# Tokens of a block in another order: turned query tiles loaded in runs of 512 bytes

## The chip, the core and the metric

The kernel runs on one core of a Trainium2 chip. The metric is the time of one execution on the device in microseconds (us); several runs of the same program are taken, and their median stands for the kernel. A difference of 0.2% (some 3.2 us here) is about the least that such a measurement can tell from none.

## What is computed

Linear attention on 8 batches x 8 heads x 576 tokens x 64 channels, then two MLPs on the 4608 x 512 tokens, all in float32:

```python
q_s = exp(q - max(q, -1)); q_s = q_s / (sum(q_s, -1) + 1e-9)
k_s = exp(k - max(k, 2));  k_s = k_s / (sum(k_s, 2) + 1e-9)
kv  = einsum('bhsd,bhse->bhde', k_s, v)
x   = einsum('bhsd,bhde->bhse', q_s, kv)     # then (token, head*64+channel), 4608 x 512
h = x @ w_in;   g = h * clip(h + 3, 0, 6) / 6;  x = g @ w_out      # first MLP, 512 -> 2048 -> 512
h = x @ w2_in;  g = h * sigmoid(h);             out = g @ w2_out   # second MLP
```

## The kernel before

The 4608 tokens are 9 blocks of 512 (`BLK`). A unit u is one block and one pair of heads, so 36 units, four per block. A block's tokens lie on the 128 partitions with four tokens each: partition p holds tokens 4p to 4p+3 (`i` in the code, `NCH` = 4). A block does not end where a batch ends (576 tokens), so `parts(j)` gives block j as one or two ranges of partitions, p0 to p0+n, each with its own batch; n is a multiple of 16.

For each unit the queries go through a softmax over the channels (`q_max`, `q_sub`, `q_exp`, `q_sum`, `q_norm`), are turned so that channels lie on partitions, and are multiplied with the batch's 128 x 128 matrix `kv` (`x_mm`, L495). The result `px` has channels on partitions and the block's 512 tokens as columns; it is the MLP's input. Up to here a token's column number is 128 i + p. Each matmul of `x_mm` reads and writes the columns of one range of partitions for all four i, as a pattern of 4 x n columns. As weights and columns are full float32, one such instruction of the program stands in the trace as two MATMUL records, each with its weight load.

The queries are turned in two ways. Units 0 to 8 use four transposes on TensorE and a copy on ACT (`q_turn`, `q_copy` L486). Units 9 to 35 use `q_blocks` (L469), a transpose on DVE that turns each 32 x 32 square in place, then `q_store` (L473), which writes the tile to DRAM (`zd`), and `q_load` (L479): four loads of 32 partitions each bring the squares to their places. In each load, one of 32 partitions takes 16 runs of 32 floats (128 bytes).

The MLPs are matmuls in which tokens stay columns: `mm1` (L541, first product), a gate on ACT and DVE (`Gate`), `mm2` (L613, L615). The first MLP of most blocks and all the attention run up to 720 us. From 720 to 1485 us five pairs of blocks go through a seven-product scheme (`inner` L1340, `outer` L1499), whose results leave over `turn_blocks` and, for the last pair, `turn_last`: DVE transposes of 32 x 32 squares and four stores each (L1547 to L1552, L1567 to L1572). The last block's second MLP is written plainly, and in its end `tail` (L637 to L652) the roles are changed: the gate's output is the weight, so a result tile has 128 tokens on partitions. `tail` makes four such tiles c, copies each in two halves (DVE and ACT, L651) and stores each half, 128 rows of 1 KB, from the queue of SP or of ACT (L652). Nothing comes after these eight stores.

The order of the work is made when the program is built: jobs with engine, guessed time and key go to the planner (`Plan`) in `middle`, events by time in `second_mlp`. Each engine then runs its list in order, and SP issues nearly all DMAs from one list; a wait there holds up what is queued behind it.

Quoted here is the one line that says how the rows of `out` belong to the columns of a tile in `tail`:

```python
rows = out[j * BLK : (j + 1) * BLK, :].rearrange("(p i) d -> i p d", i=NCH)
```

Of the kernel before, what the change touches and what calls it, by code (L numbers as in the profile page):

```python
# [18 lines left out]
P = 128  # L19
BLK = 512  # L20
# [3 lines left out]
def f32(ap):  # L24
    return ap.bitcast(F32)
# [3 lines left out]
def efficient_attention_then_two_mlps(  # L29
# [11 lines left out]
    nc = tc.nc  # L41
# [7 lines left out]
    NCH = BLK // P  # L49
# [32 lines left out]
    zd = dram.tile([NB * NP, P, NCH * P], F32, name="zd")  # L82
# [90 lines left out]
    def slot(o, i, part):  # L173
        if part == "A21":
            return 7 * NPR + i
        if o:
            return OUTER.index(part) * NPR + i
        if part == "A22":
            return 6 + 7 * i + 2 if i < NPR - 1 else 7 * NPR - 1
        return (0 if i == 0 else 6 + 7 * (i - 1)) + INNER.index(part) + (  # L180
            1 if i and part not in INNER[:2] else 0
        )
# [105 lines left out]
    qt, kv = {}, {}  # L288
    xt = {}
    live = {}  # L290
# [39 lines left out]
    def parts(j):  # L330
        p = 0
        while p < P:
            b, s = divmod(j * BLK + NCH * p, S)
            n = min(P - p, (S - s) // NCH)
            yield p, n, b, s
            p += n

    def a_psum(shape, small=False):
        t = ps_a.tile([P, 512], F32, tag="a", name="pa")
        return t  # L340
# [116 lines left out]
    def q_turn(u):  # L457
        t = live.pop(("qe", u)).rearrange("p i h d -> p i (h d)")
        pq = a_psum(None)
        for i in range(NCH):  # L460
            nc.tensor.transpose(pq[:, i * P : (i + 1) * P], t[:, i, :], ident)
        live["pq", u] = pq
# [3 lines left out]
    def q_blocks(u):  # L466
        e = live.pop(("qe", u)).rearrange("p i h d -> p (i h d)")
        z = tmp.tile([P, NCH * P], F32, tag="t2k", name="qz")
        nc.vector.transpose(z, e)  # L469
        live["z", u] = z  # L470

    def q_store(u):
# [1 line left out]

    def q_load(u):
        t = att.tile([P, NCH * P], F32, tag="qT", bufs=1, name="qt")
        zb = zd[u].rearrange("(a i) (c b k) -> b i c a k", a=4, b=4, c=NCH)
        for b in range(4):
            nc.sync.dma_start(  # L479
                t[b * 32 : b * 32 + 32].rearrange("i (c a k) -> i c a k", c=NCH, a=4), zb[b]  # L480
            )
        live["pq", u] = t

    def q_copy(u):
        t = att.tile([P, NCH * P], F32, tag="qT", bufs=1, name="qt")
        nc.scalar.copy(t, live["pq", u])  # L486
        live["pq", u] = t

    def x_mm(u):
        j, pr = divmod(u, NP)  # L490
        qt = live.pop(("pq", u)).rearrange("p (i n) -> p i n", i=NCH)
        px = a_psum(None)
        pv = px.rearrange("p (i n) -> p i n", i=NCH)
        for p0, n, b, _ in parts(j):
            nc.tensor.matmul(  # L495
                pv[:, :, p0 : p0 + n], kv[b, pr], qt[:, :, p0 : p0 + n],
                start=p0 == 0, stop=True, skip_group_check=True,
            )
        live["px", u] = px

    def x_upper(u):
# [135 lines left out]
    def tail(s):  # L637

        ph, j, f = s
        g, w = gt.pop(s), wo[ph, f]  # L640
        rows = out[j * BLK : (j + 1) * BLK, :].rearrange("(p i) d -> i p d", i=NCH)
        for c, y in enumerate(acc.pop((ph, j))):
            cs = slice(c * P, (c + 1) * P)
            for n, (a, e) in enumerate(((0, 0), (1, 0), (0, 1))):
                nc.tensor.matmul(y, g[:, e, cs], w[:, a, :], start=False, stop=n == 2)
            o = tmp.tile([P, 512], F32, tag="t2k", name="o")
            for h, (copy, eng) in enumerate(
                ((nc.vector.tensor_copy, nc.sync), (nc.scalar.copy, nc.scalar))
            ):
                half = slice(h * 256, (h + 1) * 256)  # L650
                copy(o[:, half], y[:, half])  # L651
                eng.dma_start(rows[c][:, half], o[:, half])  # L652

    def x_store(u):
        j, pr = divmod(u, NP)
# [37 lines left out]
    for i, u in enumerate(range(2, NP)):  # L693
        o = i * (KB + VB + QB)
# [15 lines left out]
    def a_pool():  # L710
        return a_psum(None)
# [109 lines left out]
    for j in range(1, NB):  # L821
        for pr in range(NP):
            n = (j - 2) * NP + pr
            begin[j * NP + pr] = 3 * pr if j == 1 else NF - 3 + int(3.3 * n) + LATE[n]

    def first_block():
# [30 lines left out]
        def unit(u, key, until=7):  # L857
# [25 lines left out]
            kx = add("ACT", 0.75, key(3), lambda: k_exp(u), [kb])  # L883
            qt_ = add("PE", 0.65, key(3), turning("q_turn", u, lambda: q_turn(u)), [qn], ["a"], [qe])
            ql = add("ACT", 0.6, key(3), lambda: q_copy(u), [qt_], ["qT"], ["a"])
            pkb = f"y{u}" if small else "a"
            mm = add(
# [4 lines left out]
            va = add("DVE", 0.35, key(4), lambda: kv_sum(u), [mm])  # L892
            vl = add("ACT", 0.65, key(4), lambda: kv_scale(u), [va], [], [pkb])
            xm = add("PE", 1.0, key(5), turning("x", u, lambda: x_mm(u)), [ql, vl], ["a"], ["qT"])
            xu = add("ACT", 0.6, key(5), lambda: x_upper(u), [xm])
            if u in DIRECT_X:
# [94 lines left out]
    def middle():  # L991
# [12 lines left out]
        def unit(u):  # L1004
# [28 lines left out]
            if u < DIRECT:  # L1033
                qt_ = add("PE", 0.65, key(3), lambda: q_turn(u), [qn], ["a"], ["qe"])
                ql = add("ACT", 0.62, key(3), lambda: q_copy(u), [qt_], ["qT"], ["a"])
            else:
                qb = add("DVE", 0.72, key(3), lambda: q_blocks(u), [qn], ["t2k"], ["qe"])
                z0 = dma(0.35, key(3), lambda: q_store(u), 256, [qb], [], ["t2k"])
                ql = dma(1.4, key(4), lambda: q_load(u), 256, [z0], ["qT", "z"])
# [269 lines left out]
    def second_mlp(last):  # L1309
# [4 lines left out]
        for _ in range(2):  # L1314
            t = raw.tile([P, 2, BLK], F32, tag="raw", name="fin")
            fixed += [t[:, 0], t[:, 1]]
        whole = xs.tile([P, 4, 2, DM], F32R, tag="x", name="ring")
# [5 lines left out]
        def small(name, tag="t2k"):  # L1323
            return tmp.tile([P, BLK], F32, tag=tag, bufs=1 if tag == "r" else 5, name=name)
# [4 lines left out]
        d = {}  # L1329
# [96 lines left out]
        def split_tile(x=False):  # L1426
            n = 2 + turns[0] % 3 if x else turns[0] % 5
            turns[0] += 1
            if n == 4:
                return [  # L1430
                    att.tile([P, BLK], F32R, tag=tag, bufs=1, name="gsp") for tag in ("ke", "qe")
                ]
            if n == 2:
                return [
                    att.tile([P, BLK], F32R, tag="sp", bufs=3, name="gsp") for _ in range(2)
                ]
            if n < 2:
                t = gs.tile([P, 2, BLK], F32R, tag="g", name="gsp")
            else:
                t = att.tile([P, 2, BLK], F32R, tag="qT", bufs=1, name="gsp")  # L1440
            return [t[:, 0], t[:, 1]]
# [94 lines left out]
        turned = []  # L1536

        def turn_blocks(j, k, part):


            h, n = (1, k) if k < NC else (0, k - NC)
            a, m = divmod(n, 2)
            x = fixed[4 * m + ((3, 1), (0, 2))[a][h]]
            if part == 0:
                if not turned:
                    turned.extend(split_tile())
                nc.vector.transpose(f32(turned[0]), x)  # L1547
            o = f32(turned[0])
            rows = out[(j + h) * BLK : (j + h + 1) * BLK, n * P : (n + 1) * P]
            e = slice(part * 32, part * 32 + 32)  # L1550
            nc.sync.dma_start(
                rows[:, e].rearrange("(b r i) c -> r i b c", b=4, i=NCH),  # L1552
                o[e].rearrange("r (i b c) -> r i b c", i=NCH, b=4),
            )
            if part == 3:
                turned.pop(0)
# [3 lines left out]
        def turn_last(j, k):  # L1560

            h, n = (1, k) if k < NC else (0, k - NC)
            a, m = divmod(n, 2)
            x = fixed[4 * m + ((3, 1), (0, 2))[a][h]]
            o = gone.pop() if k else small("o2")
            gone.append(x)
            nc.vector.transpose(o, x)  # L1567
            rows = out[(j + h) * BLK : (j + h + 1) * BLK, n * P : (n + 1) * P]
            for i in range(4):
                e = slice(i * 32, i * 32 + 32)  # L1570
                nc.sync.dma_start(
                    rows[:, e].rearrange("(b r i) c -> r i b c", b=4, i=NCH),  # L1572
                    o[e].rearrange("r (i b c) -> r i b c", i=NCH, b=4),
                )
# [4 lines left out]
        for b, (ph, j) in enumerate(PASSES):  # L1579
            t0 = T  # L1580
            place = {}
            for n in range(NPR):
                at = place[n] = {}
# [7 lines left out]
            start = {}  # L1591
# [4 lines left out]
            for n in range(NPR):  # L1596
                pair_events(b, n, place[n])
                for p, t in place[n].items():
                    k = 7 * NPR * b + slot(0, n, PAIR[p][0]) // 2
                    uses[k] = max(uses.get(k, 0.0), t)  # L1600
            for u in range(7 * NPR):
                p, i = KEYS[u // NPR], u % NPR
                t = start[u]
# [7 lines left out]
                k = 7 * NPR * b + 7 * NPR // 2 + u // 2  # L1611
# [49 lines left out]
    with tc.manual_schedule(engines=None):  # L1661
        nc.gpsimd.memset(ident, 1.0)
        nc.gpsimd.affine_select(
            out=ident, in_=ident, compare_op=ALU.is_equal, fill=0.0, base=0,
# [50 lines left out]
```

## Time and profile before

| what | value |
|---|---|
| median of 3 runs | 1578.06 us (1576.75 to 1578.68) |
| profiled execution, its own time | 1579.01 us |
| its span, first to last instruction | 1577.0 us |
| TensorE busy | 1558.9 us, 99% of the span |
| VectorE, ScalarE, GpSimd busy | 70%, 48%, 31% |
| granted clock of TensorE, mean | 1.000 |
| DMA queue of SP and ACT: packets, data, share of 16 engines | 389,040, 340.32 MB, 70.3% |

A profile shows one execution. PE is TensorE's matmuls, PEld its weight loads, DVE VectorE, ACT ScalarE, POOL GpSimd, SP the engine that issues DMAs. Busy time of an engine that is not the bottleneck costs nothing by itself; what counts is what the work that ends last waits for.

### The profile page before, as it was taken

What the parts mean: (1) busy time and instruction counts of PE and PEld (TensorE: products, weight loads), DVE (VectorE), ACT (ScalarE), POOL (GpSimd) and SP (SyncE); (2) the same over time, 40 slices, a digit from 0 to 9 for tenths busy, and PEclk for the clock granted to TensorE, in tenths of its full rate; (3) what the DMA queues carried; (4) which work ended last, traced back from release to release, by engine and by line L of the source; (5) the groups of instructions that cost most, each with busy time, mean ns of one, the idle gap of its engine ahead of it and who ended that gap; (6) DMA issues with size and microseconds to landing.
All of it is one profiled execution on the core that took longest, in us unless ns stands there. A gap on an engine that the chain in (4) does not pass through costs nothing.

```text
span 1577.0 us, 22414 instructions
## 1 busy us (share of the span) xinstructions
PE 1558.9 (99%) x7352; PEld 1268.4 (80%) x7352; DVE 1111.1 (70%) x1792; ACT 761.6 (48%) x1360; POOL 487.8 (31%) x442
## 2 busy tenths in 40 slices
PE   7999999999999999999999999999999999999998
PEld 4777878887878888888888888888888888888887
DVE  7988577776767776554689569846986697677632
ACT  6886245454555554443365236533643464345322
POOL 4334224433424335321232243323223422440000
PEclk9999999999999999999999999999999999999999
DMA  9915977777778875755666786766668875879850
GB/s 267 345 44 185 313 216 227 238 215 215 223 215 246 235 227 166 238 174 193 192 222 218 214 226 224 249 217 192 237 203 218 220 252 192 227 226 370 260 127 27
DMA packets 391203, 342.82 MB, mean 217 GB/s; under 512 B 184880, under 2 KB 297520, under 8 KB 391088
## 3 DMA queue, kind: packets, MB, share of 16 engines
q1 hardware_dynamic: 389040, 340.32, 70.3%
q8 instruction: 58, 0.95, 0.2%
q10 hardware_dynamic: 2048, 1.08, 0.2%
q14 instruction: 57, 0.47, 0.1%
HBM read 247.20 MB, written 94.11 MB: 216 GB/s over the span
## 4 chain that ended last, share of the span: by engine, by line
PE 92%; DMA 2%; issue 1%; DVE 1%; POOL 1%; ACT 1%; SPq 1%; ACTq 0%; POOLq 0%; DVEq 0%
PE pb L1340 24%; PE pb L1499 24%; PE h L541 20%; PE y L613 17%; PE y L615 3%; PE pa L495 2%; PE pa L397 2%; DMA qraw<-in_q_dram 1%; DMA xr<-xq 0%; DMA xq<-xq 0%; POOL wi L164 0%; SPq L232 0%; PE pa L368 0%; PE pa L356 0%; ACT r L554 0%
## 5 line engine op out<-in xcount | busy, mean ns | idle before, releaser
L541 PE MATMUL h<-x,wi 128*128 128x512 f32 x1536 | 382.5, 396 | 1.6 <-POOL wi L164 0.9
L1340 PE MATMUL pb<-xo,ring 128*128 128x512 f32 x1680 | 383.0, 389 | 0.0
L1499 PE MATMUL pb<-gsp,ring 128*128 128x512 f32 x1680 | 382.4, 389 | 0.0
L1340 PEld LDWEIGHTS pb<-xo,ring 128*128 128x128 f32 x1680 | 315.4, 188 | 65.8 <-issue 0.5
L1499 PEld LDWEIGHTS pb<-gsp,ring 128*128 128x128 f32 x1680 | 315.4, 188 | 65.4
L541 PEld LDWEIGHTS h<-x,wi 128*128 128x128 f32 x1536 | 283.5, 188 | 65.9 <-POOL wi L164 2.0
L613 PE MATMUL y<-g,wo 128*128 128x512 f32 x1344 | 323.9, 390 | 0.6 <-ACT g L569 0.6
L613 PEld LDWEIGHTS y<-g,wo 128*128 128x128 f32 x1344 | 251.4, 188 | 53.6 <-ACT g L569 1.1
L1327 DVE TENSOR_TENSOR gsp<-g,gsp 128x512 fp32r<-128x512 f32 x240 | 183.0, 782 | 26.0 <-ACT gsp L1445 25.2
L1445 ACT CAST gsp<-g 128x512 fp32r<-128x512 f32 x240 | 143.6, 621 | 106.2 <-PE pb L1499 88.3
L578 DVE SCALAR_TENSOR_TENSOR h<-r,h 128x512 f32<-128x512 f32 x112 | 77.4, 691 | 80.3 <-ACT r L554 80.1
L554 ACT ACTIVATE r<-h 128x512 f32<-128x512 f32 x112 | 67.0, 598 | 133.4 <-PE h L541 131.7
L1327 POOL TENSOR_TENSOR xst<-xst 128x512 f32<-128x512 f32 x32 | 72.1, 2254 | 167.4 <-DVE xo L1327 85.3
L1327 DVE TENSOR_TENSOR g<-r,pb 128x512 f32<-128x512 f32 x96 | 65.7, 684 | 54.6 <-ACT r L1354 54.1
L1354 ACT ACTIVATE r<-pb 128x512 f32<-128x512 f32 x96 | 57.1, 595 | 97.0 <-DVE pb L1327 72.8
L1327 POOL TENSOR_TENSOR g<-g 128x512 f32<-128x512 f32 x40 | 53.6, 1340 | 148.6 <-DVE g L1327 123.4
L1327 POOL TENSOR_TENSOR s<-U,s 128x512 f32<-128x512 f32 x32 | 42.6, 1331 | 173.1 <-DVE U L1327 173.1
L569 ACT CAST g<-h 128x512 fp32r<-128x512 f32 x112 | 65.6, 586 | 59.8 <-DVE h L578 51.5
L572 DVE TENSOR_TENSOR g<-h,g 128x512 fp32r<-128x512 f32 x97 | 66.7, 688 | 28.8 <-ACT g L569 27.3
L1327 DVE TENSOR_TENSOR U<-pb,s 128x512 f32<-128x512 f32 x80 | 55.0, 688 | 17.0 <-PE pb L1340 14.9
L194 POOL TENSOR_TENSOR fa<-fa 128x256 f32<-128x256 f32 x64 | 49.9, 780 | 43.7 <-DVE sp L226 28.5
L427 POOL TENSOR_TENSOR qe<-qraw,qm 128x512 f32<-128x512 f32 x34 | 37.9, 1114 | 79.4 <-DVE qz L469 46.0
(158 smaller groups left out, 1721.2 us busy)
## 6 DMA issues: line engine op xcount, KB each, us to landing
ring<-ws SPq DMA_DIRECT2D x280, 512.0 KB, 3.9
ws<-sp SPq DMA_DIRECT2D x256, 128.0 KB, 2.6
wi_early<-in_moe_w_in_dram SPq DMA_DIRECT2D x16, 512.0 KB, 8.6
wo_early<-in_moe_w_out_dram SPq DMA_DIRECT2D x16, 512.0 KB, 9.6
wi_raw<-in_moe_w_in_dram SPq DMA_DIRECT2D x16, 512.0 KB, 5.0
ws<-w_sum SPq DMA_DIRECT2D x64, 128.0 KB, 2.2
ws<-fa SPq DMA_DIRECT2D x64, 128.0 KB, 2.3
wo_raw<-in_moe_w_out_dram SPq DMA_DIRECT2D x16, 512.0 KB, 4.4
```

Of the source, the lines that this page charges most:

```text
L194: lambda to=to, x=x, y=y, op=op: nc.gpsimd.tensor_tensor(out=at[to], in0=at[x], in1=at[y], op=op)
L541: nc.tensor.matmul(h, w[:, a, c, :], x[:, e, c, :], start=(c == 0 and n == 0), stop=(c == NC - 1 and n == 2),)
L554: nc.scalar.activation(self.r, self.h, AF.Relu, bias=3.0)
L569: nc.scalar.copy(self.g[:, 0], self.r)
L572: nc.vector.tensor_tensor(out=self.g[:, 1], in0=self.r, in1=f32(self.g[:, 0]), op=ALU.subtract)
L578: nc.vector.scalar_tensor_tensor(out=self.h, in0=self.r, scalar=6.0, in1=self.h, op0=ALU.min, op1=ALU.mult)
L613: nc.tensor.matmul(y[c], w[:, a, cs], g[:, e, :], start=st, stop=sp)
L1327: (eng or nc.vector).tensor_tensor(out=out, in0=a, in1=b, op=how)
L1340: nc.tensor.matmul(to, ws_[:, a], e[:, c], start=p in ("P1", "P6", "P5") and c == 0 and m == 0, stop=c == 1 and m == 2, skip_group_check=True,
L1354: nc.scalar.activation(r, d[b, n, key], AF.Sigmoid)
L1445: nc.scalar.copy(t[0], source(p, i))
L1499: nc.tensor.matmul(d[b, p][m], w[:, a, m * P : (m + 1) * P], t[e], start=new and i == 0 and k == 0, stop=i == NPR - 1 and k == 2, skip_gro ...
```

## The change

A token's column is no longer 128 i + p. With p = 32 a + n, it is 128 a + 32 i + n: the four groups of 32 partitions come one after the other, and the four tokens of a partition stand 32 columns apart.

- `q_blocks` writes its 32 x 32 squares in the new order (pattern 4 x 4 x 32 in place of 512 elements in a row), and each load of `q_load` has 4 runs of 128 floats (512 bytes) for a partition in place of 16 runs of 32. `q_copy` gets the same reordering for units 0 to 8.
- A range of partitions p0 to p0+n is now a stretch of columns in a row as far as it takes whole groups of 32, and a pattern of 4 x 16 columns where it begins or ends in the middle of a group. `columns` gives these pieces, and `x_mm` issues one matmul for each.
- The transposes in `turn_blocks` and `turn_last` undo the order (input and output patterns 4 x 4 x 32); their stores are as before.
- `tail`: a tile c now holds group a = c, with 32 i + y on its partitions, so a store goes to rows 128 c + 4 y + i: a pattern of 4 x 32 rows in place of 128 rows with one step.

```diff
@@ -335,6 +335,19 @@
             yield p, n, b, s
             p += n
 
+    def columns(p0, p1):
+        whole = -(-p0 // 32), p1 // 32
+        out = []
+        if whole[0] < whole[1]:
+            out.append(lambda t: t[:, whole[0] * P : whole[1] * P])
+        if p0 % 32:
+            a, y = divmod(p0, 32)
+            out.append(lambda t: t[:, a * P : (a + 1) * P].rearrange("p (i y) -> p i y", i=NCH)[:, :, y:32])
+        if p1 % 32:
+            b, z = divmod(p1, 32)
+            out.append(lambda t: t[:, b * P : (b + 1) * P].rearrange("p (i y) -> p i y", i=NCH)[:, :, 0:z])
+        return out
+
     def a_psum(shape, small=False):
         t = ps_a.tile([P, 512], F32, tag="a", name="pa")
         return t
@@ -466,7 +479,9 @@
     def q_blocks(u):
         e = live.pop(("qe", u)).rearrange("p i h d -> p (i h d)")
         z = tmp.tile([P, NCH * P], F32, tag="t2k", name="qz")
-        nc.vector.transpose(z, e)
+        nc.vector.transpose(
+            z.rearrange("p (b i c) -> p i b c", b=4, i=NCH), e.rearrange("p (i b c) -> p i b c", b=4, i=NCH)
+        )
         live["z", u] = z
 
     def q_store(u):
@@ -474,28 +489,29 @@
 
     def q_load(u):
         t = att.tile([P, NCH * P], F32, tag="qT", bufs=1, name="qt")
-        zb = zd[u].rearrange("(a i) (c b k) -> b i c a k", a=4, b=4, c=NCH)
+        zb = zd[u].rearrange("(a x) (b n) -> b x a n", a=4, b=4)
         for b in range(4):
-            nc.sync.dma_start(
-                t[b * 32 : b * 32 + 32].rearrange("i (c a k) -> i c a k", c=NCH, a=4), zb[b]
-            )
+            nc.sync.dma_start(t[b * 32 : b * 32 + 32].rearrange("x (a n) -> x a n", a=4), zb[b])
         live["pq", u] = t
 
     def q_copy(u):
         t = att.tile([P, NCH * P], F32, tag="qT", bufs=1, name="qt")
-        nc.scalar.copy(t, live["pq", u])
+        nc.scalar.copy(
+            t.rearrange("p (a i n) -> p i a n", a=4, i=NCH),
+            live["pq", u].rearrange("p (i a n) -> p i a n", a=4, i=NCH),
+        )
         live["pq", u] = t
 
     def x_mm(u):
         j, pr = divmod(u, NP)
-        qt = live.pop(("pq", u)).rearrange("p (i n) -> p i n", i=NCH)
+        qt = live.pop(("pq", u))
         px = a_psum(None)
-        pv = px.rearrange("p (i n) -> p i n", i=NCH)
         for p0, n, b, _ in parts(j):
-            nc.tensor.matmul(
-                pv[:, :, p0 : p0 + n], kv[b, pr], qt[:, :, p0 : p0 + n],
-                start=p0 == 0, stop=True, skip_group_check=True,
-            )
+            for at in columns(p0, p0 + n):
+                nc.tensor.matmul(
+                    at(px), kv[b, pr], at(qt),
+                    start=p0 == 0, stop=True, skip_group_check=True,
+                )
         live["px", u] = px
 
     def x_upper(u):
@@ -638,7 +654,7 @@
 
         ph, j, f = s
         g, w = gt.pop(s), wo[ph, f]
-        rows = out[j * BLK : (j + 1) * BLK, :].rearrange("(p i) d -> i p d", i=NCH)
+        rows = out[j * BLK : (j + 1) * BLK, :].rearrange("(a y i) d -> a i y d", a=4, i=NCH)
         for c, y in enumerate(acc.pop((ph, j))):
             cs = slice(c * P, (c + 1) * P)
             for n, (a, e) in enumerate(((0, 0), (1, 0), (0, 1))):
@@ -649,7 +665,7 @@
             ):
                 half = slice(h * 256, (h + 1) * 256)
                 copy(o[:, half], y[:, half])
-                eng.dma_start(rows[c][:, half], o[:, half])
+                eng.dma_start(rows[c][:, :, half], o[:, half])
 
     def x_store(u):
         j, pr = divmod(u, NP)
@@ -1544,7 +1560,10 @@
             if part == 0:
                 if not turned:
                     turned.extend(split_tile())
-                nc.vector.transpose(f32(turned[0]), x)
+                nc.vector.transpose(
+                    f32(turned[0]).rearrange("p (i b c) -> p b i c", i=NCH, b=4),
+                    x.rearrange("p (b i c) -> p b i c", i=NCH, b=4),
+                )
             o = f32(turned[0])
             rows = out[(j + h) * BLK : (j + h + 1) * BLK, n * P : (n + 1) * P]
             e = slice(part * 32, part * 32 + 32)
@@ -1564,7 +1583,10 @@
             x = fixed[4 * m + ((3, 1), (0, 2))[a][h]]
             o = gone.pop() if k else small("o2")
             gone.append(x)
-            nc.vector.transpose(o, x)
+            nc.vector.transpose(
+                o.rearrange("p (i b c) -> p b i c", i=NCH, b=4),
+                x.rearrange("p (b i c) -> p b i c", i=NCH, b=4),
+            )
             rows = out[(j + h) * BLK : (j + h + 1) * BLK, n * P : (n + 1) * P]
             for i in range(4):
                 e = slice(i * 32, i * 32 + 32)
```

No instruction changes places with another on any engine; pieces are added and patterns changed. On PE, a unit of block 3 (ranges of 48 and 80 partitions), before, with `kv` of the two batches (pa is `px`, pa<-vbuf,ke the next unit's product of keys and values, h<-x,wi the first MLP):

```order
L541 MATMUL h<-x,wi 128x512 x12
L495 MATMUL pa<-qt,kv_96 128x4x48
L495 MATMUL pa<-qt,kv_95 128x4x80
L397 MATMUL pa<-vbuf,ke 64x65 x10
L541 MATMUL h<-x,wi 128x512 x9
```

And in the changed kernel:

```order
L557 MATMUL h<-x,wi 128x512 x12
L511 MATMUL pa<-qt,kv_96 128x128
L511 MATMUL pa<-qt,kv_96 128x4x16
L511 MATMUL pa<-qt,kv_95 128x256
L511 MATMUL pa<-qt,kv_95 128x4x16
L410 MATMUL pa<-vbuf,ke 64x65 x10
L557 MATMUL h<-x,wi 128x512 x9
```

Two matmuls have become four, with as many columns in all. Over the program there are 24 more: one more for each of the four units of blocks 1 and 7, two more for each of blocks 3 and 5, none elsewhere.

On SP, the loads of one unit, before and then in the changed kernel, with the store of the next unit's tile ahead:

```order
L473 DMA zd<-qz 128x512
L635 DMA yd<-o 128x512
L479 DMA qt<-zd 32x16x32 x4
L635 DMA yd<-o 128x512
```

```order
L488 DMA zd<-qz 128x512
L651 DMA yd<-o 128x512
L494 DMA qt<-zd 32x4x128 x4
L651 DMA yd<-o 128x512
```

The queue is the same; the four loads move the same bytes in a quarter of the runs.

On ACT, the end of the program (half of the last stores; the other four are on SP), before and then in the changed kernel:

```order
L651 COPY o<-y_13836 128x256
L652 DMA out_dram<-o 128x256
L651 COPY o<-y_13837 128x256
L652 DMA out_dram<-o 128x256
```

```order
L667 COPY o<-y_13860 128x256
L668 DMA out_dram<-o 4x32x256
L667 COPY o<-y_13861 128x256
L668 DMA out_dram<-o 4x32x256
```

The place is the same; the outermost step of the store's target has 4 entries where it had 128.

## Rows read from the trace of the kernel before

**Rows 1.** Chain of work that ended last, whole program, shares of the span.

```profile
PE 92%; DMA 2%; issue 1%; DVE 1%; POOL 1%; ACT 1%; SPq 1%; ACTq 0%; POOLq 0%; DVEq 0%
```

**Rows 2.** Windows: us, busy time of each engine (instructions), granted clock, DMA share, GB/s.

```profile
148.00:350.00 202.00, 201.56 (x1051) 162.67 (x1050) 143.37 (x261) 95.46 (x176) 74.53 (x89) 1.00 0.81 243
350.00:370.00 20.00, 19.37 (x101) 15.44 (x101) 10.29 (x20) 9.06 (x18) 10.73 (x12) 1.00 0.75 223
...
420.00:470.00 50.00, 47.40 (x241) 37.91 (x240) 35.19 (x64) 25.15 (x47) 21.91 (x25) 1.00 0.70 212
470.00:600.00 130.00, 130.00 (x672) 105.20 (x672) 95.63 (x172) 67.57 (x122) 51.14 (x58) 1.00 0.77 227
...
720.00:1485.00 765.00, 765.00 (x3375) 633.29 (x3374) 564.19 (x825) 349.43 (x614) 221.65 (x144) 1.00 0.74 231
```

**Rows 3.** Chain of work around three units' `x_mm`: start us, us, what.

```profile
652.29 0.86 PE pa L495 x2
653.15 2.75 PE h L541 x12
...
303.32 0.86 PE pa L495 x4
304.18 2.73 PE h L541 x12
...
562.75 0.92 PE pa L495 x4
563.68 2.79 PE h L541 x12
```

**Rows 4.** The same, where ten matmuls of L397 follow `x_mm`.

```profile
338.45 0.86 PE pa L495 x4
339.31 0.88 PE pa L397 x20
...
603.52 0.92 PE pa L495 x4
604.44 0.88 PE pa L397 x20
```

**Rows 5.** Lines of SP's queue, DMA issues: duration ns min/median/max, first and last start us.

```profile
L479 SPq DMA_DIRECT2D qt<-zd x108: 557/634/1432, 188.4 to 700.7; - x108
L473 SPq DMA_DIRECT2D zd<-qz x27: 319/407/589, 163.6 to 632.4; - x27
L206 SPq DMA_DIRECT2D ws<-wi x24: 576/614/1170, 137.7 to 162.3; - x24
```

**Rows 6.** Chain of work before PE's longest wait, and that wait (timeline).

```profile
451.25 0.64 SPq L479
...
452.65 2.79 DMA yd<-o
...
464.19 0.30 PE L356 MATMUL pa<-ident,peaks 128*128 128x128 f32 x1 [2.07 <-DVE peaks L351]
```

**Rows 7.** Lines of the transposes and of a DVE operation with exchanged axes: ns min/median/max.

```profile
L469 DVE STREAM_TRANSPOSE qz<-qe x27: 700/704/711, 153.1 to 630.5; 128x512 f32<-128x512 f32 x27
L377 DVE TENSOR_TENSOR ke<-kbuf,pa x28: 769/812/823, 58.3 to 606.4; 128x640 f32<-128x640 f32 x28
```

**Rows 8.** Windows of the end: columns as in rows 2.

```profile
1571.00:1572.00 1.00, 1.00 (x6) 0.82 (x5) 0.53 (x2) 0.56 (x2) 0.00 (x0) 1.00 0.14 52
1572.00:1573.00 1.00, 0.54 (x3) 0.12 (x1) 0.74 (x2) 0.54 (x2) 0.00 (x0) 1.00 0.96 332
1573.00:1574.00 1.00, 0.00 (x0) 0.00 (x0) 0.00 (x1) 0.37 (x1) 0.00 (x0) 1.00 0.95 304
1574.00:1575.00 1.00, 0.00 (x0) 0.00 (x0) 0.00 (x0) 0.00 (x0) 0.00 (x0) 1.00 1.03 336
1575.00:1576.00 1.00, 0.00 (x0) 0.00 (x0) 0.00 (x0) 0.00 (x0) 0.00 (x0) 1.00 0.08 25
```

**Rows 9.** Line L652, issues of the last eight stores on ACT, as rows 5.

```profile
L652 ACTq DMA_DIRECT2D out_dram<-o x4: 338/348/364, 1571.4 to 1573.8; - x4
```

## The prediction

> **What bounds the kernel now.** I read the chain of waits first: 92% of the span is TensorE's own matmuls, and DMA is 2% of it [rows 1]. The windows by stage say where TensorE is not full [rows 2]: from 148 to 350 us it idles 0.44 us, from 350 to 370 us 0.63 us, from 420 to 470 us 2.60 us, and nowhere in 470 to 600 or 720 to 1485 us. So two things can move the time: work added to TensorE, which is paid in full, and what stands after its last matmul. A DMA made cheaper can win back at most those 3.7 us. The loads that the change is about have little to win, although 16 engines are busy 81% of the time in 148 to 350 us. I read the end last [rows 8]: TensorE's last work ends about 1572.5 us, and then there are only the eight stores of `tail`. From 1572 to 1575 us the DMA share is 0.96, 0.95 and 1.03 at 332, 304 and 336 GB/s. So those stores do fill all 16 engines, and the end waits for them.
>
> **Pieces of `x_mm`.** 24 matmuls of the program are added, 48 in the trace, with no column more. What a piece costs I read from units that have a 4 x 16 piece today. One matmul of all 512 columns takes 0.86 us of the chain and the twelve behind it 2.75 us, 3.61 together; two of 4 x 64 take 0.86 + 2.73, so a cut in two large pieces costs nothing. Cut into 448 columns and 4 x 16, it is 0.92 + 2.79 = 3.71 us, 0.10 more [rows 3]. Where the products of keys and values follow, the pieces make it 0.92 + 0.88 against 0.86 + 0.88, 0.06 more [rows 4]. The extra pieces of the change are all of that small kind (blocks 3 and 5 have none before and two per unit after; blocks 1 and 7 have one and then two). I take 0.10 for each: 24 x 0.10 = **+2.4 us**, on the path in full. The low end is 24 x 0.06 = 1.4. In blocks 3 and 5 one small piece stands between two others and may delay both, so the high end is twice the row, 24 x 0.20 = 4.8.
>
> **Loads of `zd`.** 108 loads have a quarter of the runs. To issue one takes SP 634 ns now. The store of the same tile, with 128 runs of 2 KB, as many runs as a load will have, takes 407 ns [rows 5]. So a unit's four loads take SP about 4 x 0.23 = 0.9 us less. This matters only where SP is on the path: before TensorE's longest wait (2.07 us, at 464.19) the chain runs through the four loads and then through a store of `yd` queued behind them [rows 6]. That wait should shrink by about the same: **-1.0 us**, with a little for the lighter DMA traffic. The best case is that the idle time of 350 to 370 and 420 to 470 us all goes, -3.2. The worst is that the moved arrivals make one more wait like the longest of today, +2.1; nothing in the profile excludes that.
>
> **Transposes and copies.** The DVE transposes (27 in the attention at 704 ns, 24 in the scheme of pairs and 8 in the end) and nine copies of ACT get patterns of 4 x 4 x 32. No transpose of the trace has one. The nearest row is a subtraction on DVE with two axes exchanged, 640 elements in 812 ns, 1.27 ns each, against 704 for 512, 1.38 each, in the plain transpose [rows 7]: an exchanged order is no dearer there. I take 0. DVE is free 29% of the time from 148 to 350 us and 26% from 720 to 1485 us [rows 2], which would cover a small increase; a large one is a rival below.
>
> **The last stores.** This is the term that decides. Before, a store's target has 128 steps of one kind, and the tile has 128 partitions. Now the target's outermost step has 4 entries, with 32 rows in each, while the tile still has 128 partitions. If the queue deals a transfer to the engines by outermost steps, these eight stores can be cut into 4 parts only, and four engines carry what 16 did. The loads of `zd` do not suffer that: their outermost step is 32 partitions on both sides. The price comes from the windows [rows 8]: the shares add up to 0.14 + 0.96 + 0.95 + 1.03 + 0.08 = 3.16 us of 16 engines for the 1,049 KB that the GB/s add up to. On four engines at the same rate for each, this is 12.6 us. By the quicker of the full slices (332 GB/s at 0.96, so 86 GB/s for four engines) it is 12.1 us, by the slower (304 at 0.95, 80) 13.1. The stretch today is 3.2 us. So the end moves by 8.9 to 9.9 us. I take the quick one, **+8.9 us**, since four engines do not press each other as sixteen do. The other end of this term is that 16 engines stay at work. Then only the issue is dearer: ACT issues four of the stores in its chain of copies at 348 ns each, and the nearest issue whose two sides are laid out in different steps (the store of `wi` to `ws`, 256 runs of 1 KB) took 614 ns [rows 5, 9], so up to 4 x 0.27 = 1.1, say +0.6. A gain is excluded: rows and bytes are the same. One engine alone (50 us) is excluded as far as the step of 4 can be cut.
>
> No run here shows a DMA whose outermost step is not a multiple of 16. The Trainium skill (DMA: Bandwidth & Descriptors, section "Why a DMA increments its semaphore by 16 and not by 1") says that a DMA runs on the largest number of engines up to 16 that divides the slowest dimension of both its sides. By that rule these stores run on 4; a store that kept 16 would give the sum of the first rival.
>
> The same page (section Specifications) wants at least 512 bytes in a transfer for the line rate, which speaks for the loads. The trace bears out that they are dear to issue, not that TensorE waits for more than the 3.7 us.
>
> **Sum.** 2.4 - 1.0 + 0 + 8.9 = +10.3 us. The profiled execution took 1579.01 us (a span of 1577.0 and 2.0 around it), so it would take 1589.3. The median of the runs is 0.95 us below it: **1588.4 us**, 0.65% slower.
>
> **Rivals.** First, not slower: the eight stores keep 16 engines, because the dealing goes by the tile's 128 partitions. The place is the end after 1572 us, the price +0.6 in place of 8.9: 2.4 - 1.0 + 0.6 = +2.0, so 1580.1 us, 0.13% and not to be told from no change. It speaks for it that the tile's side is unchanged and each row is still 1 KB; against it that both sides of a transfer must be cut alike, and the target has four outer steps. It decides between 8 and 16 engines: with 8 the stores take 6.3 us, 3.1 more, and the sum is 4.5, slower. Second, the transposes cost twice as much with squares scattered, 0.70 us more each. The 27 of the attention are 19 us of DVE; if a third of that reached TensorE through late gates, it would be 6.3 us on top of the forecast: 1594.7 us. DVE's free time speaks against it, and nothing in its rows for it. Third, the shorter queue of SP ends all waits of 350 to 470 us (-3.2) and the stores keep 16 engines: 2.4 - 3.2 + 0.6 = -0.2, 1577.9 us, no change. Against it: only one of those waits has the loads in its chain. That the runs would not be 512 bytes is ruled out by the order of the changed kernel: 32 x 4 x 128 elements for a load.
>
> **How the numbers follow.** The forecast has 0.84, the first rival 0.10, the second 0.04, the third 0.02. The forecast's own range: low, pieces 1.4, waits -3.2 and stores 8.9 make 7.1, and with stores a little quicker than any slice (8.0) it is 6.2, so 1584; high, I do not add all the worst ends, but pieces 3.5, no gain from waits and stores 9.9 make 13.4, so 1591.5. That range leaves out the first and third rivals and the second, 0.16, and a little of the forecast. Slower by over 0.2% (3.2 us): the forecast, the second rival and a share of the first in which pieces cost their high end, 0.89. No change: 0.09. Faster: the rest, 0.02, where all waits go and pieces cost their low end.
>
> **What would show it.** In the windows after 1572 us, a DMA share near 0.25 at some 85 GB/s for about 12 us and a span that ends near 1586 us show the stores right; a share near 1 again shows the first rival. PE's lines should have 48 records of `x_mm` more, and the stretch up to the first matmul of the scheme of pairs should be 1 to 2 us later. The loads' issue should fall to about 0.4 us, and the 2.07 us wait to about half. Transposes away from 704 ns would show the second rival. Wrong outright would be a median below 1581.2 us, or a time grown anywhere but in `x_mm` and after the last matmul.

## The result, and the profile after

The changed kernel takes 1587.34 us (median of 4 runs, 1587.24 to 1587.99) against 1578.37 us of the kernel before in the same comparison. The ratio is 1.0059, with a 95% interval of 1.0042 to 1.0076: slower by 0.6%. The profiled execution took 1587.99 us with a span of 1586.2 us, 9.2 us longer than before.

The windows of the middle come first; they answer to [rows 2] (columns as there).

```profile
148.00:350.00 202.00, 201.47 (x1062) 163.43 (x1061) 140.67 (x264) 94.79 (x175) 75.07 (x90) 1.00 0.77 244
350.00:370.00 20.00, 20.00 (x106) 16.28 (x105) 11.33 (x21) 10.37 (x19) 11.36 (x13) 1.00 0.77 245
...
420.00:470.00 50.00, 49.70 (x258) 40.53 (x257) 35.97 (x63) 24.57 (x46) 22.09 (x25) 1.00 0.64 203
470.00:600.00 130.00, 130.00 (x673) 105.34 (x672) 96.67 (x172) 66.16 (x121) 51.85 (x59) 1.00 0.72 225
```

TensorE's idle time from 350 to 370 us is gone, and of the 2.60 us from 420 to 470 us 0.30 are left. From 148 to 350 us 0.53 us are idle, where it was 0.44. The DMA share has fallen by 0.04 to 0.06 in three of these windows and risen from 0.75 to 0.77 in the one from 350 to 370 us. The line of PE's longest wait [rows 6], in the timeline of the changed kernel:

```profile
462.96 0.30 PE L369 MATMUL pa<-ident,peaks 128*128 128x128 f32 x1 [0.29 <-DVE peaks L364]
```

The lines of the loads, of the transposes in the attention and of ACT's part of the last stores (durations ns min/median/max) answer to [rows 5, 7, 9]:

```profile
L494 SPq DMA_DIRECT2D qt<-zd x108: 303/430/1281, 189.3 to 699.5; - x108
L482 DVE STREAM_TRANSPOSE qz<-qe x27: 700/703/712, 153.8 to 630.0; 128x512 f32<-128x512 f32 x27
L668 ACTq DMA_DIRECT2D out_dram<-o x4: 544/864/1296, 1570.9 to 1574.5; - x4
```

A load is issued in 430 ns in place of 634, a transpose takes the same 703 ns, and ACT's four of the last stores are issued in 864 ns at the median in place of 348. The chain of work around `x_mm`, for a unit with one 512-column matmul, one with two small pieces at the end, and one of block 3 with two small pieces among four [rows 3, 4]:

```profile
651.79 0.86 PE pa L511 x2
652.65 2.75 PE h L557 x12
...
561.82 1.04 PE pa L511 x6
562.86 2.80 PE h L557 x12
...
243.75 1.05 PE pa L511 x8
244.80 0.88 PE pa L410 x20
```

The unit of block 3 takes 1.05 us, where the uncut 512 columns take 0.86: 0.19 for its two small pieces. The unit of block 7 (561.82) takes 1.04 + 2.80 where it took 0.92 + 2.79, 0.13 for one piece more.

Then the windows of the end, against [rows 8]:

```profile
1572.00:1573.00 1.00, 0.04 (x1) 0.00 (x0) 0.42 (x1) 0.37 (x1) 0.00 (x0) 1.00 0.24 63
1573.00:1574.00 1.00, 0.00 (x0) 0.00 (x0) 0.00 (x0) 0.37 (x1) 0.00 (x0) 1.00 0.27 90
...
1577.00:1579.00 2.00, 0.00 (x0) 0.00 (x0) 0.00 (x0) 0.00 (x0) 0.00 (x0) 0.50 0.23 53
1579.00:1581.00 2.00, 0.00 (x0) 0.00 (x0) 0.00 (x0) 0.00 (x0) 0.00 (x0) 0.50 0.27 93
1581.00:1583.00 2.00, 0.00 (x0) 0.00 (x0) 0.00 (x0) 0.00 (x0) 0.00 (x0) 0.50 0.27 96
1583.00:1584.00 1.00, 0.00 (x0) 0.00 (x0) 0.00 (x0) 0.00 (x0) 0.00 (x0) 0.50 0.27 94
1584.00:1585.00 1.00, 0.00 (x0) 0.00 (x0) 0.00 (x0) 0.00 (x0) 0.00 (x0) 0.50 0.12 43
```

The share is 0.27 at some 90 GB/s where it was 0.95 to 1.03 at 304 to 336, for about 12 us: four engines' worth, not sixteen.

To say where the 9.2 us come from, the span is cut at two places that every version has, the first `x_mm` of block 1 and the `x_mm` of the last unit. The timeline's lines for them, before and then after:

```profile
70.30 1.14 PE L495 MATMUL pa<-qt,kv 128*128 128x64 f32 x4
...
720.11 1.02 PE L495 MATMUL pa<-qt,kv 128*128 128x512 f32 x2
```

```profile
70.80 1.20 PE L511 MATMUL pa<-qt,kv 128*128 128x64 f32 x6
...
719.61 1.02 PE L511 MATMUL pa<-qt,kv 128*128 128x512 f32 x2
```

So the start is 0.5 us later (70.80 - 70.30). The middle is 1.0 us shorter: 649.81 us became 648.81. The end, from the last `x_mm` to the end of the span, is 9.7 us longer: 1577.0 - 720.11 = 856.9 became 1586.2 - 719.61 = 866.6 (the spans are given to 0.1 us). Together that is +9.2.

### The profile page after: what moved, and what is told of

Its sections match the earlier page's. It is cut to its first block, busy times and chain, and to the rows that moved or that the text cites. A ratio compares the mean times of both kernels' runs of the same rounds, so it can differ in the third digit from the quotient of the medians.

```text
span 1586.2 us, 22511 instructions
## 1 busy us (share of the span) xinstructions
PE 1563.3 (99%) x7400; PEld 1275.8 (80%) x7400; DVE 1111.3 (70%) x1792; ACT 759.9 (48%) x1360; POOL 489.5 (31%) x442
## 4 chain that ended last, share of the span: by engine, by line
PE 94%; DVE 1%; issue 1%; POOL 1%; ACT 1%; SPq 1%; DMA 0%; ACTq 0%; DVEq 0%; POOLq 0%
PE pb L1356 24%; PE pb L1515 24%; PE h L557 20%; PE y L629 18%; PE y L631 3%; PE pa L511 2%; PE pa L410 2%; POOL wi L164 0%; PE pa L474 0%; PE busy L865 0%; PE pa L381 0%; PE pk L410 0%; DMA qraw<-in_q_dram 0%; PE pa L369 0%; DMA zd<-qz 0%
```

## Experiments

All runs are compared by ratio with the kernel before, measured beside them, and by the same three stretches of their profiled executions.

**Only the shape of the last stores, on the kernel before.** The kernel before gets the store target of the changed one, with an outermost step of k = 4, and then 8 and 16:

```diff
-        rows = out[j * BLK : (j + 1) * BLK, :].rearrange("(p i) d -> i p d", i=NCH)
+        rows = out[j * BLK : (j + 1) * BLK, :].rearrange("(a y i) d -> a i y d", a=NCH, i=4)
...
-                eng.dma_start(rows[c][:, half], o[:, half])
+                eng.dma_start(rows[c][:, :, half], o[:, half])
```

> The kernel before, with the target of its last eight stores alone laid out as in the changed kernel: outermost step of 4, 32 rows in it (the rows of the last block come out permuted). Theory, dealing by outermost steps: four engines carry them, DMA share near 0.27 for some 12 us after the last matmul, and a time 9 to 10 us above before, about 1588 us. Rival, the growth came from the attention or the transposes: 1578 to 1579 us.

> The kernel before, with the target of its last eight stores in an outermost step of 8, 16 rows in it (rows of the last block permuted). Theory: eight engines, share near 0.53 for some 6.3 us, 3 to 4 us above before, about 1582 us. Rival, any target with one step more than the tile is slow by its pattern, not by its count: about 1588 us as with 4.

> The kernel before, with the target of its last eight stores in an outermost step of 16, 8 rows in it (rows of the last block permuted). Theory: all 16 engines as before, share near 1; what is left is the dearer issue (some 0.6 us in place of 0.35), 0.5 to 1.5 us above before, 1579 to 1580 us. Rival, the pattern as such is slow: about 1588 us.

Measured: 1588.93 us with 4 (ratio 1.0070, 1.0055 to 1.0085), 1581.69 us with 8 (1.0022, 1.0012 to 1.0031), 1579.34 us with 16 (1.0007, 0.9998 to 1.0017). In their windows the DMA share (the second number from the right) follows the outermost step. With 4:

```profile
1579.00:1581.00 2.00, 0.00 (x0) 0.00 (x0) 0.00 (x0) 0.00 (x0) 0.00 (x0) 0.50 0.27 89
1581.00:1583.00 2.00, 0.00 (x0) 0.00 (x0) 0.00 (x0) 0.00 (x0) 0.00 (x0) 0.50 0.27 91
```

With 8, of which these are two of about six such microseconds:

```profile
1573.00:1574.00 1.00, 0.00 (x0) 0.00 (x0) 0.00 (x0) 0.37 (x1) 0.00 (x0) 1.00 0.54 188
1577.00:1578.00 1.00, 0.00 (x0) 0.00 (x0) 0.00 (x0) 0.00 (x0) 0.00 (x0) 0.50 0.52 179
```

With 16:

```profile
1572.00:1573.00 1.00, 0.22 (x1) 0.00 (x0) 0.43 (x2) 0.36 (x2) 0.00 (x0) 1.00 0.97 288
1574.00:1575.00 1.00, 0.00 (x0) 0.00 (x0) 0.00 (x0) 0.14 (x1) 0.00 (x0) 1.00 1.01 328
```

The end is 9.7 us longer than before with 4 (1587.2 - 720.60 = 866.6), 3.1 with 8 (1579.8 - 719.79 = 860.0) and 0.7 with 16 (1577.4 - 719.81 = 857.6). The pattern as such costs little; the number of outermost steps decides. This is the whole of the end's growth, with nothing else of the change in the kernel.

The share is a mean over the 16 engines and does not say by itself how many of them work. The packets do. The profile's page counts them for each queue; ACT's is q10 (q1, whose 389,040 packets stand in the table of the kernel before, is SP's alone). Before, and then with 4, 8 and 16:

```profile
q10 hardware_dynamic: 2048, 1.08, 0.2%
q10 hardware_dynamic: 2000, 1.08, 0.2%
q10 hardware_dynamic: 2016, 1.08, 0.2%
q10 hardware_dynamic: 2048, 1.08, 0.2%
```

ACT issues four of the eight stores, so with 4 a store has 12 packets fewer than before, with 8 it has 8 fewer. In the traces these are packets of 4 bytes: beside its 128 rows of 1 KB a store leaves 4, 8 or 16 of them, and 16 before, as if each engine that has a part in it left one. By the start and length of the packets, 4 or 5 of the stores' packets are under way at once for most of the stretch with 4, 8 to 10 with 8, and up to 19 with 16. So it is fewer engines, and not sixteen that work a part of the time.

**The change with the old stores (t).** The last block's input is put back into the old order of columns where it is split for the second MLP, and `tail` is that of before:

```diff
         x, t = xt[NB + j], live.pop(("y", j, c))
-        nc.scalar.copy(x[:, 0, c, :], t)
...
+        t = t.rearrange("p (a i n) -> p a i n", a=4, i=NCH)
+        hi, lo = (x[:, k, c, :].rearrange("p (i a n) -> p a i n", a=4, i=NCH) for k in range(2))
+        nc.scalar.copy(hi, t)
+        nc.vector.tensor_tensor(out=lo, in0=t, in1=f32(hi), op=ALU.subtract)
```

> The changed kernel, in which the last block's input to the second MLP is put back into the old order of columns when it is split (four copies of ACT, four subtractions of DVE), so that the last eight stores are those of before. Theory: the 9 to 10 us of the stores go, the rest of the change stays (pieces of x_mm +2.4, less waiting), and the time is 1577 to 1579 us. Rival, that something else in the change costs several us: above 1581 us.

Measured: 1578.38 us, ratio 0.9998 (0.9989 to 1.0007), no difference from before: what the pieces cost and what the loads gain, measured below, cancel. The middle is as in the changed kernel, 719.92 - 71.08 = 648.84 us; the end is 1576.7 - 719.92 = 856.8 us, as before:

```profile
71.08 1.03 PE L511 MATMUL pa<-qt,kv 128*128 128x64 f32 x4
...
719.92 1.02 PE L511 MATMUL pa<-qt,kv 128*128 128x512 f32 x2
```

**The stores cut by their step of 4 (a_split).** Sixteen stores of 32 rows in place of eight of 4 x 32:

```diff
-                eng.dma_start(rows[c][:, :, half], o[:, half])
+            for i, eng in enumerate((nc.sync, nc.scalar) * 2):
+                eng.dma_start(rows[c][i], o[i * 32 : i * 32 + 32])
```

> The changed kernel with the last stores cut by their step of 4: sixteen stores of 32 rows of 2 KB, half on SP and half on ACT, in place of eight. Theory: 32 rows on both sides go to 16 engines, so the 9 to 10 us go, and eight more issues of some 0.35 us give back 1 to 2 of them: 1578.5 to 1580.5 us. Rival, that the scattered rows of the new order are slow by themselves: above 1584 us.

Measured: 1580.37 us, ratio 1.0006 (0.9997 to 1.0015). The end is 1579.2 - 720.43 = 858.8 us, 1.9 longer than before. So the same scattered rows, cut so that both sides have 32 steps, cost little. The 1.9 us fit the eight added issues, but here a store also waits for both halves of its tile, and no run separates the two. Putting the order right beforehand, as in t, costs nothing that the end shows.

**The pieces (t_cut).** Run t with the old cut of `x_mm`, two patterns for a unit in place of up to four:

```diff
-            for at in columns(p0, p0 + n):
-                nc.tensor.matmul(
...
+            at = lambda t: t.rearrange("p (i n) -> p i n", i=NCH)[:, :, p0 : p0 + n]
+            nc.tensor.matmul(
```

> The changed kernel with the last stores of before (run t), in which x_mm cuts its columns as before: two patterns of 4 x n in place of the pieces, 24 matmuls fewer (columns go to the wrong batch's matrix where a batch begins inside a block; nothing else changes). Theory: the pieces cost 0.06 to 0.20 us each on TensorE's path, so the blocks that have them (1, 3, 5, 7) are 1.4 to 4.8 us shorter in all than in t, and the time is 1575 to 1577 us. Rival, that pieces lie in waits or cost nothing: 1578 us as in t.

Measured: 1575.72 us, ratio 0.9977 (0.9967 to 0.9986). The middle is 717.12 - 70.55 = 646.57 us against 648.84 in t:

```profile
70.55 1.14 PE L511 MATMUL pa<-qt,kv 128*128 128x64 f32 x4
...
717.12 1.02 PE L511 MATMUL pa<-qt,kv 128*128 128x512 f32 x2
```

The 24 pieces cost 2.27 us, 0.095 each; the ratios (0.9977 against 0.9998) say 3.3, with intervals of some 1.5 us on either. TensorE's idle time from 148 to 600 us is about the same in both (1.0 us in t_cut, 0.9 in t), so this is work and not waiting.

**The loads.** The old loads in run t (t_short), and the new loads in the kernel before (b_load). The edit of b_load; that of t_short is its reverse:

```diff
-        zb = zd[u].rearrange("(a i) (c b k) -> b i c a k", a=4, b=4, c=NCH)
+        zb = zd[u].rearrange("(a x) (b n) -> b x a n", a=4, b=4)
         for b in range(4):
-            nc.sync.dma_start(
-                t[b * 32 : b * 32 + 32].rearrange("i (c a k) -> i c a k", c=NCH, a=4), zb[b]
-            )
+            nc.sync.dma_start(t[b * 32 : b * 32 + 32].rearrange("x (a n) -> x a n", a=4), zb[b])
```

> Run t with the loads of before alone: 16 runs of 128 bytes for a partition (columns of the units from 9 on come out permuted). Theory: the loads take SP 0.63 us each again and the waits of 350 to 470 us come back, 1 to 3.2 us above t, 1579 to 1581 us. Rival, that the loads' runs do nothing for TensorE: 1578 us as in t.

> The kernel before with the loads of the change alone: 4 runs of 512 bytes for a partition (columns of the units from 9 on come out permuted). Theory: the waits of 350 to 470 us shrink and nothing is added, 1 to 3.2 us below before, 1575 to 1577 us. Rival, that the loads' runs do nothing for TensorE: 1578 us as before.

Measured: t_short 1580.42 us, ratio 1.0011 (1.0002 to 1.0019); b_load 1575.51 us, ratio 0.9975 (0.9966 to 0.9984). In b_load the middle is 717.03 - 70.36 = 646.67 us:

```profile
70.36 1.14 PE L493 MATMUL pa<-qt,kv 128*128 128x64 f32 x4
...
717.03 1.02 PE L493 MATMUL pa<-qt,kv 128*128 128x512 f32 x2
```

That is 3.1 us less than the 649.81 of before; the three kernels with k = 4, 8 and 16, whose middle is that of before, have 649.80, 649.10 and 649.68, so this stretch repeats to some 0.7 us. In t_short it is 721.24 - 70.52 = 650.72 us, 1.9 more than in t. So the loads are worth 1.9 to 3.1 us by the middles, and 2.1 and 3.9 by the ratios. TensorE's idle time from 148 to 600 us shows the larger part of it as waiting: 2.07 us in t_short against 0.89 in t, and 1.04 in b_load against 3.67 before. The waits of t_short are not those of before, though: they are 1.13 us from 148 to 350 and 0.94 from 420 to 470.

**What of a load it is (b_issue).** Run b_load with three tiny loads more for each unit:

```diff
             nc.sync.dma_start(t[b * 32 : b * 32 + 32].rearrange("x (a n) -> x a n", a=4), zb[b])
+            if b < 3:
+                nc.sync.dma_start(extra[b], q[0, 0, 0:32, 0:4])
```

> Run b_load with three tiny loads (32 partitions x 16 bytes into tiles that nothing reads) behind the first three loads of each unit, so that SP spends about as long on a unit as in the kernel before, some 0.3 us for each, while the traffic of the loads stays light. Each also takes one of the eight places that DMAs in flight have (a DMA waits for the one eight before it on its semaphore). Theory A, the gain of b_load is SP's time: it goes, 1577 to 1579 us. Theory B, it is the lighter traffic, so that other DMAs land sooner: the time stays at 1575 to 1576 us. If it goes, A is not separated from the places in flight.

Measured: 1587.06 us, ratio 1.0045 (1.0033 to 1.0057), against 0.9975 of b_load some 11 us more: neither theory's number. The tiny loads took 428 ns each, so 1.3 us for a unit instead of the 0.9 meant, and `x_mm` now waited for its loads. All of the growth lies in the middle, 729.96 - 70.49 = 659.47 us, 12.8 more than in b_load:

```profile
PE pa L496 <- DMA qt<-zd: 3.4, 2, 2.8
L482 SPq DMA_DIRECT2D extra<-in_q_dram x81: 331/428/1785, 192.0 to 710.7; - x81
...
70.49 1.14 PE L496 MATMUL pa<-qt,kv 128*128 128x64 f32 x4
...
729.96 1.02 PE L496 MATMUL pa<-qt,kv 128*128 128x512 f32 x2
```

TensorE idles 9.7 us from 148 to 600 us, against 1.0 in b_load; the two waits for the loads are 3.4 us of that, and the rest of the 12.8 us is not accounted for here. The tiny loads move 41 KB in all, so SP's list alone can set TensorE's time in the attention. Whether by the time of its issues or by the places in flight is not separated, and the share that the lighter traffic has in the gain of b_load stays open as well.

**A version below both (g16).** Run t with groups of 16 partitions, so that no range of partitions is cut in pieces (the edit against t, shortened):

```diff
-            for at in columns(p0, p0 + n):
...
+            at = slice(NCH * p0, NCH * (p0 + n))
+            nc.tensor.matmul(
+                px[:, at], kv[b, pr], qt[:, at],
...
-            z.rearrange("p (b i c) -> p i b c", b=4, i=NCH), e.rearrange("p (i b c) -> p i b c", b=4, i=NCH)
+            z.rearrange("p (m i c) -> p i m c", m=8, i=NCH), e.rearrange("p (i m c) -> p i m c", m=8, i=NCH)
```

> Run t with groups of 16 partitions in place of 32: a token's column is 64 (p div 16) + 16 i + (p mod 16), the loads of queries keep their 512-byte runs, and since every batch begins at a multiple of 16 partitions, each range of partitions is one stretch of columns and x_mm has as many matmuls as in the kernel before. The transposes write runs of 16. Theory: loads -2 to -4 us, no pieces, stores as before: 1574.5 to 1576.5 us, below both kernels. Rival, transposes that write runs of 16 are dearer (above 704 ns): up to 1578 us or more.

Measured: 1575.40 us, ratio 0.9977 (0.9967 to 0.9986), faster than the kernel before by 0.23% and than the changed one by 0.8%. The middle is 717.82 - 71.25 = 646.57 us, as in t_cut, and a transpose that writes runs of 16 takes 704 ns:

```profile
71.25 1.14 PE L498 MATMUL pa<-qt,kv 128*128 128x64 f32 x4
...
717.82 1.02 PE L498 MATMUL pa<-qt,kv 128*128 128x512 f32 x2
...
L469 DVE STREAM_TRANSPOSE qz<-qe x27: 699/704/712, 154.1 to 628.2; 128x512 f32<-128x512 f32 x27
```

## Why the prediction was right

The forecast was 1588.4 us for the median, within 1584.0 to 1591.5; it is 1587.34. The forecast case came, and the terms were measured one by one. That the sum is only 1.1 us off is in part luck: the loads gave more than forecast and the stores cost more, and the two misses partly cancel.

| term | forecast | measured | by |
|---|---|---|---|
| pieces of `x_mm` | +2.4 | +2.3 | t against t_cut, middle |
| waits that the loads' change ends | -1.0 | -1.9 to -3.1 | t_short against t; b_load against before; idle time in the changed kernel -2.8 |
| transposes and copies | 0 | 0 | their lines: 703 ns; g16 704 ns |
| last stores | +8.9 | +9.7 | end of the span; b4 gives the same |
| sum | +10.3 | +8.97 by the medians, +9.2 by the spans | |

**The pieces** held: 0.095 us each, where a row of the same small piece had given 0.10. TensorE's records of `x_mm` went from 128 to 176, 48 more as said.

**The loads** were the term of the sum that was mis-sized, by 1 to 2 us. The step that failed is "That wait should shrink by about the same: -1.0 us, with a little for the lighter DMA traffic." The issue did fall as said (430 ns against 407 supposed), but the idle time did not shrink by SP's 0.9 us: over the windows of [rows 2] up to 600 us it went from 3.67 to 0.83 us, 2.8 less, near the best case of -3.2. So the statement that the scheme of pairs would begin 1 to 2 us later was wrong: the last unit's `x_mm` came 0.5 us earlier.

What was wrong in the step is that I priced one wait of one execution. b4, b8 and b16 run the attention of the kernel before, and their waits lie elsewhere. The windows of b4:

```profile
148.00:350.00 202.00, 200.14 (x1043) 160.98 (x1042) 141.95 (x263) 94.99 (x175) 75.00 (x88) 1.00 0.80 241
350.00:370.00 20.00, 20.00 (x105) 16.29 (x104) 11.92 (x21) 9.51 (x19) 11.28 (x13) 1.00 0.84 244
...
420.00:470.00 50.00, 48.84 (x249) 39.43 (x248) 35.97 (x62) 24.90 (x46) 21.93 (x25) 1.00 0.69 209
470.00:600.00 130.00, 129.45 (x669) 104.53 (x668) 95.29 (x171) 66.85 (x122) 51.10 (x58) 1.00 0.76 226
```

It idles 1.86 us where before idled 0.44, nothing from 350 to 370 us, and 1.16 us where before idled 2.60. What repeats is the sum from 148 to 600 us: 2.8 to 3.7 us in these four kernels (2.07 in t_short, which has the pieces too), and 0.8 to 1.0 in the six kernels with the new loads alone or with the rest of the change (the changed one, t, t_cut, a_split, b_load, g16). The chain before the idle 0.63 us at 367 us says how such a wait comes about without the loads of `zd` in it:

```profile
348.16 0.42 SPq L232
...
350.19 5.28 DMA xq<-xq
...
359.54 5.48 DMA xr<-xq
...
367.94 2.11 PE y L613 x8
```

It runs through SP's list (from 345.64 to 350.14 us) and through two transfers that took 5.3 and 5.5 us, where such transfers land after 2.4 and 3.2 us at the median. Which of the two the new loads ease, the list or the traffic, stays open.

**The last stores** were the term that decided, and the reason for it is shown: 4, 8 and 16 outermost steps give shares of 0.27, 0.54 and 1, and 9.7, 3.1 and 0.7 us. The estimate by the quicker slice, 12.1 us for the stretch, was short by about one: the transfers run from the 0.06 share of 1571 us to some 1585 us, 13 us, with a dip to 53 GB/s from 1577 to 1579 us that b4 shows too (23 GB/s from 1578 to 1579 us) and no run explains. The reason given for the quicker slice, that four engines do not press each other as sixteen do, is not borne out: a packet of 1 KB of these stores took 48 ns on average before and 52 in the changed kernel, 46 at the median in both. The Trainium skill (DMA: Bandwidth & Descriptors, "Why a DMA increments its semaphore by 16 and not by 1") says that a DMA uses the largest number of engines up to 16 that divides the slowest dimension of both sides. The trace agrees: shares of 0.27, 0.54 and 1 for 4, 8 and 16.

**The rivals.** The first (16 engines stay) falls with the windows of the end. The second (dearer transposes) falls with 703 ns. The third had its first half right: most of the waits did go, though whether by SP's shorter queue is not shown.

**The start**, 0.5 us, cannot be told from the spread: kernels with the same beginning (before, b4, b8 and b16) reach the first `x_mm` of block 1 between 70.13 and 70.80 us. Those with the changed beginning (the changed one, t, t_cut, t_short and a_split) reach it between 70.52 and 71.42, so some tenths may belong to the change.

## What to carry to other kernels

A change of layout reaches every transfer that crosses it: go through all of them, and write down for each the outermost step on both sides, since in these runs that number said how many engines share the work. The store with 128 partitions on one side and 4 steps on the other ran on four engines; where nothing follows that hides it, put the order right earlier, in an operation that is made anyway and takes a pattern for nothing (here a copy and a subtraction per tile). And where short waits come and go from run to run, price the idle time of the whole stretch, from more than one trace if there is one, and not the longest wait of one execution.

## What was not expected

- The list of SP is much closer to TensorE's path than its waits of 3.7 us told: 81 tiny loads of 512 bytes cost some 11 us (b_issue against b_load).
- The issue of a store itself grew, and not evenly. ACT's four issues took 1.15, 0.58, 0.54 and 1.30 us in the changed kernel, and 1.14, 0.57, 0.54 and 1.31 in b4, so the median of 864 ns stands between two kinds. With 8 steps only the first is long (1.22 us, then 0.61 to 0.64), with 16 none is. That a store's engines are still busy does not explain it: the two short issues of the changed kernel stand between the long ones, with the same four engines at work. The end did not wait for it, since the stores' transfers ran on to 1585 us, and no run tries it alone. The line of the run with 16:

```profile
L652 ACTq DMA_DIRECT2D out_dram<-o x4: 546/558/634, 1571.1 to 1574.2; - x4
```
